# Inverse 16-point step of a spectral layer on 64x64 quarters of the array, two units at once, its outer level of signs moved to the finished rows

## The chip, the core and the metric

One core of a Trainium2 chip runs the whole program. The metric is the device time of one execution in microseconds, and smaller is better. Engines are named as the profile names them: PE (TensorE, matrix products), PEld (its weight loads), DVE (VectorE), ACT (ScalarE), POOL (GpSimd), SP (SyncE, which issues the transfers).

## The reference

The kernel adds a spectral layer and an MLP to its input. Sequence length S is 2048, width D is 512, hidden width F is 1792.

```python
xn = _layernorm(x, axis=-1)
# spectral part
X = jnp.fft.rfft2(xn, axes=(-2, -1)) * (w_r + 1j * w_i)
y = jnp.fft.irfft2(X, s=(S, D), axes=(-2, -1))
# MLP part
h = jnp.einsum("bsd,df->bsf", xn, w1) + b1
m = jnp.einsum("bsf,fd->bsd", h * jnp.tanh(softplus(h)), w2)
return x + y + m
```

## The kernel before

**Precision.** Every float32 operand is split into a float16 high and low half, and a product is three matmuls: high by high, high by low, low by high. The helper `mm3` (L61, L64, L65) issues them into one PSUM tile.

**The spectral part** does the Fourier transform along the sequence as 128 x 16 and goes through these steps: `s1_mm` (128-point transform for each of 16 residues s2), `p2_unit` (16-point step, PSUM tile psP2), `spectrum` (transform along the width into dre and dim, unpacking X, product with the weights w, result u), `dp_unit` (inverse along the width, psA, result `at`, moved into `ai` by four transfers), `ip_unit` (inverse 16-point step, psT, result `tt`, written to the DRAM array d_t by two transfers) and `s1_inverse` (inverse 128-point transform, psY, added into the output rows m or y). There are four chunks c of four units each, so 16 units of the 16-point steps, numbered 4c+g, and 16 calls of `s1_inverse`. `spectrum` runs twice for a chunk, for the even and the odd columns (par 0 and 1).

**An `ip_unit`** is three matmuls of 128 x 128 constants (`c_ip2`) against 512 columns of `ai`; the constants hold the whole 16-point transform. In its unit 0 one block of 128 columns has other constants, so that it has six matmuls. Its result leaves PSUM by an ACT operation (L626, high half) and a DVE operation (L627, low half).

**The MLP** runs as a row of half tiles. A half tile is `up(n)` (12 matmuls of 512 columns into ph, then the activation on ACT, hb and a, and the low half of a on DVE) or `down(n)` (12 matmuls of 512 columns into four tiles pa). There are 109 before the end, and the last four end the sum (pe). `mlp_end` adds pa into the rows m or y on DVE when a group of 512 rows is complete.

**The order** around the change is made by `stream_a` and a scheduler. `stream_a` is a generator that issues the spectral steps and yields their weights; after each yield the main loop issues as many MLP half tiles as keep the count of half tiles in step with the sum of the weights, so that `stream_a` ends at half tile B_END = 98. An `ip_unit` is issued when more than two units wait in the list `mid`. After it, `load_yi` issues 16 loads from d_t, one for each `s1_inverse`, and the calls of `s1_inverse` are spread over what is left of the half tiles, the first T_LAG = 5 of them behind. Engines take their instructions in program order. Tiles psP2, dre, dim, psA, psT and psY all use the PSUM pool ps_f, which has two buffers.

Of the kernel before, what the change touches and what calls it, by code (L numbers as in the profile page):

```python
# [19 lines left out]
P = 128  # L20
# [3 lines left out]
LAG = 2  # L24
N_UNITS = 101
LAST = 3
B_END = 98
T_LAG = 5
T_HOLD = 2


O_P2, O_IP2, O_D, O_I = 0, 512, 1024, 2048
N_CM = 3072


@with_exitstack
def spectral_mlp_kernel(ctx, tc, x, wt, w0, w1, b1, w2, cT, cIT, cM, out):
    nc = tc.nc
# [7 lines left out]
    tp = ctx.enter_context(tc.tile_pool(name="tp", bufs=1))  # L46
# [7 lines left out]
    outv = out.rearrange("(p s) d -> p s d", s=NS2)  # L54

    d_y1 = dp.tile([64, P, 256], F16, tag="d_y1", name="d_y1")
    d_t = dp.tile([P, 64, 256], F16, tag="d_t", name="d_t")

    def mm3(ps, stat, mov, start, stop, order=False):

        first = nc.tensor.matmul(ps, stat(0), mov(0), start=start, stop=False)  # L61
        if order:
            tc.keep_in_program_order(first)
        nc.tensor.matmul(ps, stat(0), mov(1), start=False, stop=False)  # L64
        nc.tensor.matmul(ps, stat(1), mov(0), start=False, stop=stop)  # L65
# [192 lines left out]
    sc = {}  # L258
# [180 lines left out]
    def load_yt(c, b, n=1):  # L439
        t = big.tile([P, 2, 4, 2, P], F16, tag="big", name=f"yt_{c}_{b}")  # L440
        w = 2048 // n
        for k in range(n):
            o = (2 * c + b) * 2048 + k * w
            tc.keep_in_program_order(
                nc.sync.dma_start(
                    t.rearrange("p g a h e -> p (g a h e)")[:, k * w : (k + 1) * w],
                    d_y1.rearrange("a (c f) e -> (a c) (f e)", c=2)[:, o : o + w],
                )
            )
        yts.setdefault(c, []).extend([t[:, 0], t[:, 1]])  # L450
# [161 lines left out]
                    at[:, k].rearrange("p h e -> p (h e)"),  # L612
                )

    def ip_unit(c, g):
        if True:
            fg = 4 * c + g
            ai = ait.pop(fg)
            ps = ps_f.tile([P, 4, P], F32, tag="f", name=f"psT_{fg}")
# [5 lines left out]
            tt = tp.tile([P, 4, 2, P], F16, tag="q2", name=f"tt_{fg}", bufs=3)  # L625
            nc.scalar.mul(tt[:, :, 0, :], ps, 2.0**-12)  # L626
            nc.vector.scalar_tensor_tensor(  # L627
                tt[:, :, 1, :], ps, 2.0**-12, tt[:, :, 0, :], op0=ALU.mult, op1=ALU.subtract
            )
            for c2 in range(2):  # L630
                f = 64 * c2 + 4 * fg
                nc.sync.dma_start(
                    d_t[f : f + 4].rearrange("f s e -> s f e"),
                    tt[64 * c2 : 64 * c2 + 64].rearrange("p l h e -> p l (h e)"),
                )


# [125 lines left out]
    def load_yi(todo):  # L763
        spots = []
        for tag in ("z", "u"):
            t = tp.tile([P, 4, 4, 2, P], F16, tag=tag, name=f"yi_{tag}")
            spots += [t[:, k] for k in range(4)]
        for k in range(4):
            t = tp.tile([P, 2, 4, 2, P], F16, tag=f"w{k}", name=f"yi_w{k}")
            spots += [t[:, 0], t[:, 1]]  # L770
        for (g, s), t in zip(todo, spots):
            nc.sync.dma_start(t.rearrange("p a h e -> p (a h e)"), d_t[:, 4 * (4 * g + s) : 4 * (4 * g + s) + 4].rearrange("p a e -> p (a e)"))
            yis.append(t)

    def s1_inverse(g, s):
        s2 = 4 * g + s
        yi = yis.pop(0)
        ps = ps_f.tile([P, 4, P], F32, tag="f", name=f"psY_{s2}")
        psr = ps.rearrange("p (b a) e -> p a b e", a=2)

        def slots(h, a):
            v = yi[:, :, h, :].rearrange("p (b a) e -> p a b e", a=2)[:, a]
            return v[:, :, ::-1] if a else v

        for a in range(2):
            mm3(psr[:, a], lambda h: sc["cIT"][:, s2, h, :], lambda h: slots(h, a), True, True, a == 0)
        psf = ps.rearrange("p a b -> p (a b)")
        if g in macc:
            m = macc[g][:, s, :]
            nc.vector.scalar_tensor_tensor(m, psf, sc["k"], m, op0=ALU.mult, op1=ALU.add)  # L790
            nc.sync.dma_start(outv[:, s2, :], m)
        else:
            if s % 2 == 0:
                sc["y"] = big.tile([P, 2, D], F32, tag="big", name=f"y_{s2}")
                nc.sync.dma_start(sc["y"], xv[:, s2 : s2 + 2, :])
            y = sc["y"][:, s % 2, :]
            nc.vector.scalar_tensor_tensor(y, psf, sc["k"], y, op0=ALU.mult, op1=ALU.add)
            yacc.setdefault(g, []).append(y)


# [7 lines left out]

    def stream_a():
        up_, mid = [], []  # L810
        load_yt(0, 0, 2)
        load_yt(0, 1, 2)
        for c in range(5):
            for g in range(4):
                if g in (1, 2) and c < 4:
                    load_wx(c, g - 1)
                if c < 4:
                    p2_unit(c, g)
                    yield 0.7
                if len(mid) > 2:  # L820
                    ip_unit(*mid.pop(0))
                    yield 0.7
            up_ += [(c - 1, g) for g in range(4)] if c else []
            if c == 1:
                load_it()
            if c < 4:
                for par in range(2):
                    if c < 3:
                        load_yt(c + 1, par)
                    for wgt in spectrum(c, par):  # L830
                        yield wgt
                        if up_:
                            u = up_.pop(0)
                            dp_unit(*u)
                            mid.append(u)
                            yield 0.7
                        elif len(mid) > 2:
                            ip_unit(*mid.pop(0))
                            yield 0.7
        while up_ or mid:  # L840
            if up_:
                u = up_.pop(0)
                dp_unit(*u)
                mid.append(u)
                yield 0.7
            if len(mid) > 2 or not up_:
                ip_unit(*mid.pop(0))
                yield 0.7

    ACT, DVE, POOL = nc.scalar, nc.vector, nc.gpsimd  # L850
# [409 lines left out]
def _dft_constants():  # L1260
# [11 lines left out]
    s = np.arange(16)  # L1272
# [109 lines left out]
```

## Time and profile before

| what | value |
|---|---|
| median of 3 runs | 370.63 us (370.26 to 370.74) |
| the profiled execution, its own time | 370.42 us |
| its span in the profile | 368.6 us |
| instructions | 5647 |
| PE, DVE, ACT, POOL busy | 362.0, 250.4, 171.6, 46.4 us |

The profile shows one execution. Its page gives busy times by engine, the span in 40 slices, the DMA queues, the chain of work that ended last, and the costliest groups of instructions; a row of a group reads line, engine, operation, output<-inputs, shapes and count, then busy time and the mean of one in ns, then the idle time of the engine just before and what ended it. A row of the timeline reads start, duration, engine, line, operation, tiles, shape and count; a wait stands in brackets with what ended it. A PE row's duration is longer than the distance to the next start, since matmuls are pipelined. Rows of SP (SPq) are issues of transfers. A row of the windows reads the stretch, its length, and for PE, PEld, DVE, ACT and POOL the busy time with the count, then the clock and the DMA share.

### The profile page before, as it was taken

To read this page: it belongs to the slowest core of one execution; us is meant where nothing else is said; L and a number is where in the kernel's file an instruction comes from. 1 tells how busy PE (TensorE), PEld (TensorE's weight loads), DVE (VectorE), ACT (ScalarE), POOL (GpSimd) and SP (SyncE) were. 2 spreads that over 40 slices of the span, in tenths; PEclk is the share of its full clock that TensorE was granted. 3 is DMA by queue.
4 is the path that set the end of the run, shared out by engine and by line. 5 is a ranking of instruction groups with operands and counts; after the bars stand their busy time and mean duration, and the time that the engine had idled before them with its cause. 6 is when DMAs were issued, how large, how long until landed. Compare 5 with 4: busy or idle time off the path is not lost.

```text
span 368.6 us, 5647 instructions
## 1 busy us (share of the span) xinstructions
PE 362.0 (98%) x2088; PEld 185.0 (50%) x2088; DVE 250.4 (68%) x474; ACT 171.6 (47%) x260; POOL 46.4 (13%) x49
## 2 busy tenths in 40 slices
PE   6999999999999999999999999999999999999996
PEld 2544445544544455444555454544545444445654
DVE  4898999643477654589887856877479944413454
ACT  5989968416335343342454354345435444422100
POOL 0020003202304200303030303030030300000000
PEclk9999999999999999999999999999999999999999
DMA  8935543896483488037202370106921234549554
GB/s 280 317 121 205 216 135 84 166 363 183 134 236 93 119 186 286 0 116 275 68 17 64 92 220 12 47 20 177 308 81 52 65 86 103 127 87 325 217 190 181
DMA packets 56011, 55.78 MB, mean 151 GB/s; under 512 B 16128, under 2 KB 44704, under 8 KB 55216
## 3 DMA queue, kind: packets, MB, share of 16 engines
q1 hardware_dynamic: 55984, 55.43, 49.7%
q8 instruction: 16, 0.26, 0.3%
q14 instruction: 11, 0.09, 0.1%
HBM read 35.46 MB, written 12.58 MB: 130 GB/s over the span
## 4 chain that ended last, share of the span: by engine, by line
PE 93%; DVE 2%; DMA 2%; SPq 1%; ACT 1%; issue 0%; ACTq 0%; DVEq 0%
PE ph L659 39%; PE pa L64 13%; PE pa L65 13%; PE pa L61 13%; PE psP L470 1%; PE psY L61 1%; DMA x<-in_x_dram 1%; PE psY L64 1%; PE psP L480 1%; PE psY L65 1%; PE psT L61 1%; DMA ai<-at 1%; PE psT L65 1%; PE psT L64 1%; PE psA L61 1%; PE psA L64 1%
## 5 line engine op out<-in xcount | busy, mean ns | idle before, releaser
L659 PE MATMUL ph<-xnT,w1t 128*128 128x512 f16 x672 | 153.7, 379 | 0.0
L659 PEld LDWEIGHTS <-w1t 128*128 128x128 f16 x672 | 65.0, 98 | 74.4 <-ACT w1t L304 0.3
L670 ACT ACTIVATE hb<-ph,b1t,fp_exp 128x512 f32<-128x512 f32 x56 | 43.2, 772 | 76.9 <-PE ph L659 76.9
L65 PE MATMUL pa<-w2t,a 128*128 128x512 f16 x181 | 68.6, 379 | 0.0
L61 PE MATMUL pa<-w2t,a 128*128 128x512 f16 x181 | 68.6, 379 | 0.0
L64 PE MATMUL pa<-w2t,a 128*128 128x512 f16 x181 | 68.6, 379 | 0.0
L682 DVE SCALAR_TENSOR_TENSOR a<-hb,ip_a,a 128x512 f16<-128x512 f32 x46 | 36.0, 783 | 35.9 <-ACT a L679 35.7
L679 ACT ACTIVATE a<-hb,ip_a 128x512 f16<-128x512 f32 x46 | 33.1, 719 | 2.2 <-DVE ip_a L243 1.2
L65 PEld LDWEIGHTS <-a 128*128 128x128 f16 x190 | 18.6, 98 | 21.1
L61 PEld LDWEIGHTS <-a 128*128 128x128 f16 x190 | 18.6, 98 | 19.3
L64 PEld LDWEIGHTS <-a 128*128 128x128 f16 x190 | 18.6, 98 | 19.0
L627 DVE SCALAR_TENSOR_TENSOR tt<-psT,tt 128x512 f16<-128x512 f32 x16 | 11.0, 687 | 17.7 <-ACT tt L626 17.7
L204 POOL TENSOR_TENSOR xh<-xs,xh 128x512 f16<-128x512 f32 x12 | 14.8, 1233 | 63.9 <-ACT xh L188 32.5
L485 DVE SCALAR_TENSOR_TENSOR z<-psP,z 128x512 f16<-128x512 f32 x16 | 10.9, 690 | 13.6 <-ACT z L484 13.6
L626 ACT ACTIVATE tt<-psT 128x512 f16<-128x512 f32 x16 | 9.5, 591 | 17.4 <-PE psT L65 13.9
L603 ACT ACTIVATE at<-psA 128x512 f16<-128x512 f32 x16 | 9.4, 589 | 17.0 <-PE psA L65 15.9
L379 ACT ACTIVATE u<-w,sc_u 128x512 f16<-128x512 f32 x16 | 10.8, 714 | 11.1 <-DVE w L579 7.0
L604 DVE SCALAR_TENSOR_TENSOR at<-psA,at 128x512 f16<-128x512 f32 x16 | 11.0, 687 | 7.2 <-ACT at L603 7.1
L188 ACT ACTIVATE xh<-x,nb,rs 128x512 f16<-128x512 f32 x12 | 9.7, 804 | 12.9 <-DVE nb L182 12.9
L484 ACT ACTIVATE z<-psP 128x512 f16<-128x512 f32 x16 | 9.5, 594 | 12.3 <-PE psP L480 12.3
L97 ACT ACTIVATE y<-psS 128x512 f16<-128x512 f32 x16 | 9.4, 588 | 11.3 <-PE psS L65 11.3
L98 DVE SCALAR_TENSOR_TENSOR y<-psS,y 128x512 f16<-128x512 f32 x16 | 11.0, 686 | 5.3 <-ACT y L97 5.3
(205 smaller groups left out, 569.7 us busy)
## 6 DMA issues: line engine op xcount, KB each, us to landing
wm<-in_wt_dram SPq DMA_DIRECT2D x8, 512.0 KB
ai<-at SPq DMA_DIRECT2D x64, 64.0 KB
d_t<-tt SPq DMA_DIRECT2D x32, 128.0 KB
w1s<-in_w_dram SPq DMA_DIRECT2D x7, 512.0 KB
w2s<-in_w_dram SPq DMA_DIRECT2D x7, 512.0 KB
d_y<-y SPq DMA_DIRECT2D x7, 512.0 KB
m<-in_x_dram SPq DMA_DIRECT2D x3, 1024.0 KB
yt<-d_y SPq DMA_DIRECT2D x6, 512.0 KB
```

Source lines behind the costliest of these rows:

```text
L61: first = nc.tensor.matmul(ps, stat(0), mov(0), start=start, stop=False)
L64: nc.tensor.matmul(ps, stat(0), mov(1), start=False, stop=False)
L65: nc.tensor.matmul(ps, stat(1), mov(0), start=False, stop=stop)
L98: nc.vector.scalar_tensor_tensor(y1v[:, :, 1, :], psv, 2.0**-17, y1v[:, :, 0, :], op0=ALU.mult, op1=ALU.subtract)
L204: engine.tensor_sub(self.xh[s][:, 1, :], self.xs[s], self.xh[s][:, 0, :])
L485: nc.vector.scalar_tensor_tensor(zl, psv, 2.0**-14, zh, op0=ALU.mult, op1=ALU.subtract)
L604: nc.vector.scalar_tensor_tensor(at[:, :, 1, :], ps, 2.0**-15, at[:, :, 0, :], op0=ALU.mult, op1=ALU.subtract)
L627: nc.vector.scalar_tensor_tensor(tt[:, :, 1, :], ps, 2.0**-12, tt[:, :, 0, :], op0=ALU.mult, op1=ALU.subtract)
L659: nc.tensor.matmul(ph[n + k], w1t[:, hw, dc, f * P : (f + 1) * P], xnT[g][:, hx, dc, :], start=(hw, hx, dc) == (0, 0, 0), stop=(hw, hx, dc ...
L670: nc.scalar.activation(hbt[n], ph.pop(n), AF.Mish, bias=b1t[:, f : f + 1], scale=s_exp[part_of(f)])
L679: nc.scalar.activation(act[n][:, 0, :], hbt[n], AF.Copy, scale=sc["a"])
L682: nc.vector.scalar_tensor_tensor(act[n][:, 1, :], hbt.pop(n), sc["a"], act[n][:, 0, :], op0=ALU.mult, op1=ALU.subtract)
```

## The change

The 16 calls of `ip_unit` become eight calls of `ip_pair`. The constants become two 64 x 64 blocks, one for each half r of the partitions of `ai`: each gives a part of the 16-point transform without its outermost sum and difference. A pair takes two units u. For each of the three products it issues four matmuls of 64 x 64 by 512 columns, one for each (u, r): the weights and `ai` from partition half r, the result into partition half u of the PSUM tile r. So a tile psT holds half r of both units and no longer one whole unit. Its two parts go to d_t[0] and d_t[1]. Unit 0's special block is six quarter matmuls of 128 columns more.

`load_yi` fetches the two parts for each `s1_inverse` with two transfers of 64 partitions where there was one of 128. `s1_inverse` has the same matmuls, and then adds the parts into the finished rows: the first part into both halves of 256 columns, the second with a plus into the lower and a minus into the upper half. That makes three DVE operations (512, 256 and 256 columns) where there was one (512). A scalar `nk` holds the negative factor.

The schedule changes too: `stream_a` ends at half tile 93, T_LAG is 4, a pair is issued behind the first `p2_unit` of a chunk or in `spectrum` where no `dp_unit` waits, and a yield of 0 ahead of each pair and behind it issues one half tile there.

```diff
-B_END = 98
-T_LAG = 5
+B_END = 93
+T_LAG = 4
...
+P2_AT, SP_AT = 0, 0
...
-    d_t = dp.tile([P, 64, 256], F16, tag="d_t", name="d_t")
+    d_t = dp.tile([2, 64, 64, 256], F16, tag="d_t", name="d_t")
...
-    c_ip2 = cMt[:, O_IP2 : O_IP2 + 512].rearrange("p (v h q) -> p v h q", v=2, h=2)
+    c_ip2 = cMt[:, O_IP2 : O_IP2 + 256].rearrange("p (v h q) -> p v h q", v=2, h=2)
...
+        sc["nk"] = scalars("nk", pW, -(2.0**-16))
...
-            if fg == 0:
-                mm3(ps[:, 0], lambda h: c_ip2[:, 1, h, :], lambda h: ai[:, 0, h, :], True, True, True)
-                mm3(ps[:, 1:4], lambda h: c_ip2[:, 0, h, :], lambda h: ai[:, 1:4, h, :], True, True)
-            else:
-                mm3(ps, lambda h: c_ip2[:, 0, h, :], lambda h: ai[:, :, h, :], True, True, True)
...
+    def ip_pair(c, g):
+
+        fgs = (4 * c + g, 4 * c + g + 1)
+        ai = [ait.pop(fg) for fg in fgs]
+        ps = [ps_f.tile([P, 4, P], F32, tag="f", name=f"psT_{fg}") for fg in fgs]
+        tiles = [(u, r) for u in (1, 0) for r in (1, 0)]
+        passes = ((0, 0), (0, 1), (1, 0))
+
+        def quarter(u, r, k, v, ls):
+            hc, hm = passes[k]
+            qs = slice(64 * r, 64 * r + 64)
+            return nc.tensor.matmul(
+                ps[r][64 * u : 64 * u + 64, ls],
+                c_ip2[qs, v, hc, :],
+                ai[u][qs, ls, hm, :],
+                start=k == 0,
+                stop=k == 2,
+            )
...
+        for k in range(3):
+            for t in tiles:
+                i = rest(k, *t)
...
+            for u in range(2):
+                f = 4 * fgs[u]
                 nc.sync.dma_start(
-                    d_t[f : f + 4].rearrange("f s e -> s f e"),
-                    tt[64 * c2 : 64 * c2 + 64].rearrange("p l h e -> p l (h e)"),
+                    d_t[r, f : f + 4].rearrange("f q e -> q f e"),
+                    tt[64 * u : 64 * u + 64].rearrange("p l h e -> p l (h e)"),
...
+            for c2 in range(2):
+                q = 32 * c2 + 2 * s2
+                nc.sync.dma_start(
+                    t[64 * c2 : 64 * c2 + 64].rearrange("p (r a) h e -> p r (a h e)", r=2),
+                    d_t[:, :, q : q + 2].rearrange("r f a e -> f r (a e)"),
+                )
...
+        def add_to(m):
+            mv = m.rearrange("p (b q) -> p b q", b=2)
+            nc.vector.scalar_tensor_tensor(
+                mv, psv[:, 0:1].to_broadcast((P, 2, 256)), sc["k"], mv, op0=ALU.mult, op1=ALU.add
+            )
+            for b, k in ((0, "k"), (1, "nk")):
+                nc.vector.scalar_tensor_tensor(mv[:, b], psv[:, 1], sc[k], mv[:, b], op0=ALU.mult, op1=ALU.add)
...
+        def pair():
+            yield 0
+            ip_pair(*mid.pop(0))
+            mid.pop(0)
+            yield 0
+            yield 1.4
...
+                if g == P2_AT and mid:
+                    yield from pair()
...
-                        elif len(mid) > 2:
-                            ip_unit(*mid.pop(0))
-                            yield 0.7
+                        elif n == SP_AT and len(mid) > 2:
+                            yield from pair()
...
+            if len(mid) > 3 or not up_:
+                yield from pair()
...
+        if not w:
+            half_tile()
+            continue
...
-        inv.append(np.einsum("dk,csaj->kajcsd", e, M).reshape(128, 128))
+        inv.append(
+            np.concatenate(
+                [np.einsum("dk,csaj->kajcsd", e[:2, 2 * r : 2 * r + 2], M).reshape(64, 64) for r in range(2)]
+            )
+        )
```

Before, PE did unit 8 like this, in the middle of the last chunk's work (psT is written from `ai` of the unit and the constants in cMt; w1t and xnT behind it belong to a half tile `up`):

```order
L61 LDWEIGHTS cMt_87
L61 MATMUL psT_8_3162<-ai_8_2897,cMt_87 128x512
L64 LDWEIGHTS cMt_87
L64 MATMUL psT_8_3162<-ai_8_2897,cMt_87 128x512
L65 LDWEIGHTS cMt_87
L65 MATMUL psT_8_3162<-ai_8_2897,cMt_87 128x512
L61 LDWEIGHTS a_3_2_2878
L61 MATMUL pa_3_0_3051<-w2t_90,a_3_2_2878 128x512
```

In the changed kernel units 8 and 9 stand together on PE, behind one half tile; the first pass and the first matmul of the second are shown:

```order
L628 LDWEIGHTS cMt_87
L628 MATMUL psT_9_3096<-ai_9_2944,cMt_87 64x512
L628 LDWEIGHTS cMt_87
L628 MATMUL psT_8_3095<-ai_9_2944,cMt_87 64x512
L628 LDWEIGHTS cMt_87
L628 MATMUL psT_9_3096<-ai_8_2896,cMt_87 64x512
L628 LDWEIGHTS cMt_87
L628 MATMUL psT_8_3095<-ai_8_2896,cMt_87 64x512
L628 LDWEIGHTS cMt_87
L628 MATMUL psT_9_3096<-ai_9_2944,cMt_87 64x512
```

Six rows for one unit, each matmul on 128 rows, have become 24 for two units, each on 64; the two tiles psT take turns, and both are written from both units.

DVE before, at the last `spectrum` (chunk 3, odd columns): X is unpacked from dre and es (a copy of dim), multiplied by the weights wO into w, summed, and written as u:

```order
L546 TENSOR_TENSOR X1_3_3077<-dre1_3_3067,es1_3_3075 128x256
L547 TENSOR_TENSOR X1_3_3077<-dre1_3_3067,es1_3_3075 128x256
L548 TENSOR_TENSOR X1_3_3077<-dre1_3_3067,es1_3_3075 128x256
L549 TENSOR_TENSOR X1_3_3077<-es1_3_3075,dre1_3_3067 128x256
L553 TENSOR_TENSOR w0_1_3_3109<-X1_3_3077,wO_3_2790 128x512
L627 SCALAR_TENSOR_TENSOR tt_6_3086<-psT_6_3082,tt_6_3086 128x4x128
L555 TENSOR_TENSOR w1_1_3_3110<-X1_3_3077,wO_3_2790 128x512
L559 TENSOR_TENSOR w2_1_3_3111<-w2_1_3_3111,w3_1_3_3112 128x512
L557 TENSOR_TENSOR w0_1_3_3109<-w0_1_3_3109,w1_1_3_3110 128x512
L682 SCALAR_TENSOR_TENSOR a_3_5_3106<-hb_3_5_3104,ip_a_379,a_3_5_3106 128x512
L567 TENSOR_TENSOR w1_1_3_3110<-w0_1_3_3109 128x4x64
```

DVE in the changed kernel at the same place; m_2 are the rows of group 2, to which `mlp_end` adds the four tiles pa:

```order
L548 TENSOR_TENSOR X1_3_3056<-dre1_3_3046,es1_3_3054 128x256
L549 TENSOR_TENSOR X1_3_3056<-dre1_3_3046,es1_3_3054 128x256
L550 TENSOR_TENSOR X1_3_3056<-dre1_3_3046,es1_3_3054 128x256
L551 TENSOR_TENSOR X1_3_3056<-es1_3_3054,dre1_3_3046 128x256
L732 SCALAR_TENSOR_TENSOR m_2_2718<-pa_2_1_2045,s_out_576,m_2_2718 128x512
L732 SCALAR_TENSOR_TENSOR m_2_2718<-pa_2_2_2046,s_out_576,m_2_2718 128x512
L732 SCALAR_TENSOR_TENSOR m_2_2718<-pa_2_3_2047,s_out_576,m_2_2718 128x512
L555 TENSOR_TENSOR w0_1_3_3137<-X1_3_3056,wO_3_2807 128x512
L557 TENSOR_TENSOR w1_1_3_3138<-X1_3_3056,wO_3_2807 128x512
L561 TENSOR_TENSOR w2_1_3_3139<-w2_1_3_3139,w3_1_3_3140 128x512
L706 SCALAR_TENSOR_TENSOR a_3_3_3092<-hb_3_3_3090,ip_a_379,a_3_3_3092 128x512
L651 SCALAR_TENSOR_TENSOR tt_8_3109<-psT_8_3095,tt_8_3109 128x4x128
```

The three rows m from pa_2_1 to pa_2_3 now stand between X and its products; before, `mlp_end` of that group stood ahead of X. The a and both tt of the pair now come between the products and their sum w0.

PE before, at the first unit that reads this u (psA of unit 12), with what stands ahead of it:

```order
L61 MATMUL psT_9_3205<-ai_9_2955,cMt_87 128x512
L64 LDWEIGHTS cMt_87
L64 MATMUL psT_9_3205<-ai_9_2955,cMt_87 128x512
L65 LDWEIGHTS cMt_87
L65 MATMUL psT_9_3205<-ai_9_2955,cMt_87 128x512
L61 LDWEIGHTS u_3_2834
L61 MATMUL psA_12_3214<-cMt_87,u_3_2834 128x128
L64 LDWEIGHTS u_3_2834
L64 MATMUL psA_12_3214<-cMt_87,u_3_2834 128x128
L65 LDWEIGHTS u_3_2834
```

PE in the changed kernel at the same unit, from its sixth matmul on:

```order
L66 MATMUL psA_12_3171<-cMt_87,u_3_2839 128x128
L62 LDWEIGHTS u_3_2839
L62 MATMUL psA_12_3171<-cMt_87,u_3_2839 128x128
L65 LDWEIGHTS u_3_2839
L65 MATMUL psA_12_3171<-cMt_87,u_3_2839 128x128
L683 LDWEIGHTS w1t_89
L683 MATMUL ph_3_5_3192<-xnT_3_1145,w1t_89 128x512
```

Before, unit 12 came whole behind a psT, with five half tiles between it and dim of the last `spectrum`; now the scheduler has put three matmuls of `up` into it, and it stands three half tiles, one pair and eight matmuls of a fourth behind dim.

More of the change, by code (lines that the diff above doesn't have):

```diff
@@ L613, in dp_unit, with rest @@
                 )
[L615 to L619, printed above, removed]
-            if fg == 0:
-                mm3(ps[:, 0], lambda h: c_ip2[:, 1, h, :], lambda h: ai[:, 0, h, :], True, True, True)
-                mm3(ps[:, 1:4], lambda h: c_ip2[:, 0, h, :], lambda h: ai[:, 1:4, h, :], True, True)
-            else:
-                mm3(ps, lambda h: c_ip2[:, 0, h, :], lambda h: ai[:, :, h, :], True, True, True)
-            tt = tp.tile([P, 4, 2, P], F16, tag="q2", name=f"tt_{fg}", bufs=3)
-            nc.scalar.mul(tt[:, :, 0, :], ps, 2.0**-12)
+    def ip_pair(c, g):
[14 more added lines that the diff above has]
+            )
+        def rest(k, u, r):
+            return quarter(u, r, k, 0, slice(1 if fgs[u] == 0 else 0, 4))
+        for k in range(3):
+            for t in tiles:
+                i = rest(k, *t)
+                if (k, t) == (0, tiles[0]):
+                    tc.keep_in_program_order(i)
+        if fgs[0] == 0:
+            for k in range(3):
+                for r in range(2):
+                    quarter(0, r, k, 1, slice(0, 1))
+        for r in range(2):
+            tt = tp.tile([P, 4, 2, P], F16, tag="q2", name=f"tt_{fgs[r]}", bufs=3)
+            nc.scalar.mul(tt[:, :, 0, :], ps[r], 2.0**-12)
@@ L771, in load_yi @@
         for (g, s), t in zip(todo, spots):
[L772 removed]
+            s2 = 4 * g + s
+            for c2 in range(2):
[4 more added lines that the diff above has]
+                )
             yis.append(t)
@@ L796, in s1_inverse @@
             y = sc["y"][:, s % 2, :]
-            nc.vector.scalar_tensor_tensor(y, psf, sc["k"], y, op0=ALU.mult, op1=ALU.add)
+            add_to(y)
             yacc.setdefault(g, []).append(y)
@@ L813, in stream_a @@
         for c in range(5):
-            for g in range(4):
-                if g in (1, 2) and c < 4:
+            for g in range(4 if c < 4 else 0):
+                if g in (1, 2):
                     load_wx(c, g - 1)
-                if c < 4:
-                    p2_unit(c, g)
-                    yield 0.7
-                if len(mid) > 2:
-                    ip_unit(*mid.pop(0))
-                    yield 0.7
+                p2_unit(c, g)
+                yield 0.7
+                if g == P2_AT and mid:
+                    yield from pair()
             up_ += [(c - 1, g) for g in range(4)] if c else []
@@ L829, in stream_a @@
                         load_yt(c + 1, par)
-                    for wgt in spectrum(c, par):
+                    for n, wgt in enumerate(spectrum(c, par)):
                         yield wgt
```

17 lines of the change are left out of this document (5 added, 12 removed).

## Prediction

> **What bounds the kernel now.** I read the page first: the busy shares, the granted clock and the shares of the chain that ended last.
>
> ```profile
> PE 362.0 (98%) x2088; PEld 185.0 (50%) x2088; DVE 250.4 (68%) x474; ACT 171.6 (47%) x260; POOL 46.4 (13%) x49
> ...
> PEclk9999999999999999999999999999999999999999
> ...
> PE 93%; DVE 2%; DMA 2%; SPq 1%; ACT 1%; issue 0%; ACTq 0%; DVEq 0%
> ```
>
> TensorE is the bound: it is busy for 98% of the span, at the full clock in every slice, and 93% of the chain is its own. A busy PE need not be at its peak, so the next view is the timeline around one inverse 16-point step (unit 15, PSUM tile psT; PEld is the weight load).
>
> ```profile
> 324.86 0.38 PE L61 MATMUL psT<-ai,cMt 128*128 128x512 f16 x1
> 324.87 0.10 PEld L64 LDWEIGHTS <-cMt 128*128 128x128 f16 x1
> 325.08 0.38 PE L64 MATMUL psT<-ai,cMt 128*128 128x512 f16 x1
> 325.08 0.10 PEld L65 LDWEIGHTS <-cMt 128*128 128x128 f16 x1
> 325.30 0.38 PE L65 MATMUL psT<-ai,cMt 128*128 128x512 f16 x1
> ...
> 325.51 0.38 PE L659 MATMUL ph<-xnT,w1t 128*128 128x512 f16 x1
> ```
>
> The reader should see three things. Starts are 0.216 us apart, so a unit holds PE for 3 x 0.216 = 0.65 us. A matmul's row lasts 0.38, so some 0.16 of each (its tail) lies under the next one. And a weight load starts with the matmul ahead of it and is over before that one ends: loads cost nothing here. Any PE time taken away shortens the kernel, unless PE then waits for something else.
>
> **What the change removes.** Sixteen units at 0.65 become eight pairs. A pair issues 12 matmuls on quarters of the array, three passes of four. If the four of a pass run side by side, a pass takes what one 512-column matmul takes, and a pair 3 x 0.216 = 0.65 where two units took 1.29. Eight times 0.65 is **5.2 us saved**. Unit 0 has a column block with other constants; here is what it costs now:
>
> ```profile
> 205.82 0.22 PE L61 MATMUL psT<-ai,cMt 128*128 128x128 f16 x1
> ...
> 205.99 0.33 PE L61 MATMUL psT<-ai,cMt 128*128 128x384 f16 x1
> ...
> 206.48 2.75 PE L659 MATMUL ph<-xnT,w1t 128*128 128x512 f16 x12
> ```
>
> Three 128-column matmuls take 0.17 and the unit 0.66 like any other. After the change its other columns run beside unit 1's full 512 and save nothing more, and six 128-column quarters, two at a time, add 0.17. The removal is worth **-5.0**.
>
> **Going into the quarters and out again.** The trace holds no matmul of 64 rows, so the price of a change of array shape, 16 in all, has to be bounded. Below: nothing, or a gain of nothing, since no work goes away with it. Above: the tail of the matmul ahead (0.16) and one weight load in the open (0.10), 0.26 each, 4.2 in all. Neither row is nearer than the other, so I take the middle, 0.13 each: **+2.1**, and a pair of 0.91.
>
> **A new wait, at the last spectrum.** The two order excerpts on DVE show it. The block that ends with u (the input of units 12 to 15) starts from the matmuls dim of PE, and these are its rows now in the timelines of PE, POOL, DVE and ACT:
>
> ```profile
> 287.32 0.38 PE L65 MATMUL dim<-z,cMt 128*128 128x512 f16 x1
> ...
> 289.24 1.27 POOL L554 TENSOR_TENSOR w<-X,wO 128x512 f32<-128x512 f32 x1 [16.10 <-issue]
> ...
> 289.35 0.41 DVE L549 TENSOR_TENSOR X<-es,dre 128x256 f32<-128x256 f32 x1
> 289.68 1.38 DVE L553 TENSOR_TENSOR w<-X,wO 128x512 f32<-128x512 f32 x1
> ...
> 290.46 1.72 POOL L556 TENSOR_TENSOR w<-X,wO 128x512 f32<-128x512 f32 x1
> ...
> 291.58 1.15 DVE L555 TENSOR_TENSOR w<-X,wO 128x512 f32<-128x512 f32 x1
> ...
> 293.26 0.68 DVE L557 TENSOR_TENSOR w<-w,w 128x512 f32<-128x512 f32 x1
> ...
> 295.19 0.41 DVE L569 TENSOR_TENSOR w<-w 128x256 f32<-128x256 f32 x1
> ...
> 295.70 1.34 ACT L379 ACTIVATE u<-w,sc_u 128x512 f16<-128x512 f32 x2 [0.89 <-DVE w L569]
> ...
> 279.59 2.07 DVE L708 SCALAR_TENSOR_TENSOR m<-pa,s_out,m 128x512 f32<-128x512 f32 x3
> ```
>
> Count from the start of the last dim. Now the upper halves of u are there at 295.70 + 1.34 - 287.32 = 9.7. After the change three rows m stand between X and w (last line: 2.07 for three). X ends at 2.4, m at 4.5. Both products then run mostly after POOL's two (1.9 to 4.9), so they cost 0.68 like the other wide ones and not 1.38 and 1.15: with some overlap left, 6.1. Then one wide sum (6.7), one a and two tt at 0.65 (8.7), the other sum (9.3), the quarter operations (third at 10.3) and ACT's two (11.65). PE, meanwhile, has 44 matmuls of 0.216, dim itself, the pair and six of 0.055 in front of the first matmul that reads this u: 9.5 + 0.2 + 0.91 + 0.33 = 10.95. It waits 0.7, and 0.2 more for a lower half, which DVE makes behind an a: **+0.9**. Bounds: 0, if DVE runs earlier than I add it up, and 2.5, if the products keep their old 1.38 and 1.15.
>
> **Other waits of PE.** Two go, both at psT in the stretch where SyncE issues the ai and d_t transfers back to back:
>
> ```profile
> 304.17 0.38 PE L65 MATMUL pa<-w2t,a 128*128 128x512 f16 x1
> 304.67 0.38 PE L61 MATMUL psT<-ai,cMt 128*128 128x512 f16 x1
> ...
> 311.89 0.38 PE L61 MATMUL pa<-w2t,a 128*128 128x512 f16 x1
> 312.54 0.38 PE L61 MATMUL psT<-ai,cMt 128*128 128x512 f16 x1 [0.27 <-DVE tt L627]
> ```
>
> The starts are 0.50 and 0.65 apart instead of 0.216: 0.28 + 0.43 = **-0.7**, since every pair now has a half tile (12 matmuls, 2.6) ahead of it and one behind. In exchange a pair takes both buffers of ps_f at once, and its transfers come in blocks (two groups of the page, a piece of the chain, a row of SyncE's timeline):
>
> ```profile
> L627 DVE SCALAR_TENSOR_TENSOR tt<-psT,tt 128x512 f16<-128x512 f32 x16 | 11.0, 687 | 17.7 <-ACT tt L626 17.7
> ...
> L626 ACT ACTIVATE tt<-psT 128x512 f16<-128x512 f32 x16 | 9.5, 591 | 17.4 <-PE psT L65 13.9
> ...
> 307.89 3.10 DMA ai<-at
> ...
> 314.73 2.51 SPq L610 DMA_DIRECT2D ai<-at  x4
> ```
>
> A buffer comes free behind an ACT and a DVE operation (0.6 and 0.7), the second one 0.6 later: 1.9 after the pair, which the half tile covers as long as neither engine has over half a microsecond queued. On SyncE the four stores of pair 10 and 11 (0.63 each) and the eight ai of units 14 and 15 stand in a row; counted from the end of that pair the stores end at 4.0, the first ai can start at 4.8 (behind psA of unit 14, ACT and DVE), and the last is issued at 9.8 and has landed by 12.9 at the 3.1 above, which is a landing in a crowd. The last pair starts at 3.9 + 3 x 2.6 + 0.9 = 12.6: covered but for 0.3. With psP2 and dim set at new places the cover will not hold everywhere; for some five places I take **+1.2**, between 0.3 (five at under 0.1) and 2.
>
> **The finished rows.** Every s1_inverse gets two more DVE operations of 256 columns, and the first keeps its 512.
>
> ```profile
> L790 DVE SCALAR_TENSOR_TENSOR m<-psY,sc_k,m 128x512 f32<-128x512 f32 x12 | 8.5, 743 | 4.6 <-PE psY L65 4.6
> L753 DVE SCALAR_TENSOR_TENSOR y<-pe,s_out,y 128x256 f32<-128x256 f32 x1 | 0.5, 483 | 0.2 <-PE pe L65 0.2
> ...
> 330.00:369.00 39.00, 35.25 (x228) 21.36 (x226) 17.34 (x26) 4.50 (x6) 0.00 (x0) 1.00 0.61 217
> ```
>
> 32 x 0.48 is at most 15.5 us of DVE, which in its last stage has 17.3 busy (the third sum of the last line) of 39, and the stage gets longer by five half tiles (13 us). PE hides it; without that cover a psY would wait about 1 us (two more operations) for its buffer. At the very end DVE has 2 us more to do while PE does its last 36 matmuls (nine of 512 columns, nine of 256, eighteen of 128: 1.9 + 1.0 + 1.0): **+0.2**, between 0 and 0.6. Loading the finished parts takes 32 transfers and not 16, on SyncE:
>
> ```profile
> 327.06 1.85 SPq L632 DMA_DIRECT2D d_t<-tt  x2
> 330.85 1.76 SPq L772 DMA_DIRECT2D yi_z<-d_t  x4
> ```
>
> At 0.44 an issue the extra sixteen cost SyncE 7 us, spread over the stage; the first unit needs one more issue and two more stores, some 2 us, and has five half tiles (13 us) before it, where it had three. Nothing, unless the loads are slow by several us.
>
> **Sum:** -5.0 + 2.1 + 0.9 - 0.7 + 1.2 + 0.2 = **-1.3**. The profiled execution took 370.42, which gives 369.1; the median of the runs is 370.63, 0.2 higher, so 369.1 to 369.3. About 0.2%, 0.74 us, is what a measurement can tell from no change.
>
> **Rivals.**
> *A, the quarters overlap but the array is emptied at each change and loads stand in the open.* Per pair the tail twice, and five loads (four for the quarters, one on the way out), of 0.05 to 0.10 since they have half the columns: 0.57 to 0.82, 4.6 to 6.5 in all. The wait at u shrinks to about 0.5. Sum +0.8 to +2.7: 371.2 to 373.1, slower. It decides from 0.21 per change on, where the sum is zero. For it: the loads' rows show them ahead of time only within one shape. Against it: the change between 128, 384 and 512 columns costs nothing above.
> The Trainium skill, page TensorEngine Tiling (Array Packing), Tiling Modes, Key Properties, says that changing the mode drains TensorE, and its Gotcha 2 that column tiling excludes the fast weight load; by that rule A holds. No row here shows it.
> *B, the waits eat the gain.* Half way to the upper bounds at u and at the other places (1.7 and 1.6) the sum is -0.1, 370.3, and at them (2.5 and 2) +1.1, 371.5: mostly no change. For it: DVE is the second busiest engine and gets 15 us more.
> *C, the change does not do what it says: quarters follow one another.* 96 x 0.216 = 20.7 instead of 10.4: +10.4 and more, some 382; if two of four overlap, nothing is saved and about 374. For it: no row shows two matmuls at once. Against it: the four read and write disjoint partitions and banks, so nothing in the program orders them.
> The Trainium skill, page TensorE: Matmul & The Clock Gate, Part 3, has packed matmuls of different tiles start about 4 ns apart; by it C falls and a pass is 0.23. No row here shows that either.
>
> **Chances.** Forecast (367.0 to 369.9) 0.57; A 0.20; B 0.15; C 0.08. The range reaches from 367.0 (no price for the change of shape, a wait at u of 1.1 since PE gets there sooner: -5.0 + 1.1 - 0.7 + 1.2 = -3.4) to 372.6; it leaves out C and the far end of A. Faster: the forecast, 0.57. Same: B and the near end of A, 0.15 + 0.02. Slower: 0.18 + 0.08 = 0.26.
>
> **What would show it.** The four quarter rows of a pass should start within 0.05 of one another and the next pass 0.22 later; from the first quarter to the next full matmul 0.65 to 1.2 (the row's start minus 0.216 of the one ahead gives the price in, the start of ph behind it the price out). The first psA of unit 12 that reads new u should start about 0.7 late. psT at 304 and 312 should start without a wait. DVE should be some 13 us busier after 325 with no psY late. Quarters 0.2 apart would be C; a pair over 1.3, A.

## The result, and the profile after

The changed kernel takes 368.24 us, the median of runs between 368.07 and 368.45; the kernel before takes 370.63 (370.26 to 370.74) beside it. The ratio is 0.9937, with an interval of 0.9920 to 0.9955. Run again beside the last experiments it took 368.78 (368.51 to 369.66), ratio 0.9954 (0.9940 to 0.9967). The forecast was 369.1, with a range of 367.0 to 372.6, and faster as the likeliest case. The result lies well inside that range, which was wide, near its fast end. The profiled execution took 368.08, its span 366.3; against 370.42 that is 2.34 less, where the sum said 1.3.

From the page of the changed kernel: the span, the busy shares, the granted clock, the chain that ended last by engine.

```profile
span 366.3 us, 5788 instructions
...
PE 360.1 (98%) x2139; PEld 182.3 (50%) x2139; DVE 259.7 (71%) x507; ACT 172.0 (47%) x260; POOL 45.8 (13%) x49
...
PEclk9999999999999999999999999999999999999999
...
PE 83%; DVE 11%; DMA 2%; ACT 2%; issue 1%; SPq 1%; ACTq 0%; DVEq 0%
```

PE is still the bound at the full clock. But the chain has 11% of DVE in it where it had 2%: part of the end time is now set by what PE waits for. The pair of units 10 and 11 in the timelines of PE and of the weight loads:

```profile
296.07 0.38 PE L66 MATMUL pa<-w2t,a 128*128 128x512 f16 x1
296.38 0.36 PEld L628 LDWEIGHTS <-cMt 64*64 64x64 f16 x12 [0.42 <-DMA ai<-at]
296.38 0.84 PE L628 MATMUL psT<-ai,cMt 64*64 64x512 f16 x12
...
297.15 2.12 PE L683 MATMUL ph<-xnT,w1t 128*128 128x512 f16 x9
```

And the same timeline of PE cut at 296.40, so that only what had started by then is in it:

```profile
296.38 0.41 PE L628 MATMUL psT<-ai,cMt 64*64 64x512 f16 x4
```

One quarter's row in a first pass is 0.40 long, and the row of the four together 0.41: they have started within 0.01 and run side by side. The first starts 0.31 behind the matmul ahead instead of 0.216, which is 0.09 on the way in. From it to the first full matmul behind the pair are 0.77, where three passes of 0.216 would be 0.65: 0.10 on the way out, and some 0.02 in the first pass. The pair costs 0.87 of PE, two units cost 1.29. The pair of units 0 and 1 has six more matmuls, those of 128 columns for unit 0's special block, and still lasts only 0.78, so they cost next to nothing:

```profile
203.98 0.85 PE L628 MATMUL psT<-ai,cMt 64*64 64x512 f16 x18
204.76 0.39 PE L62 MATMUL pa<-w2t,a 128*128 128x512 f16 x1
```

The last spectrum in the timelines of all engines; the last dim on PE starts the block:

```profile
278.39 0.38 PE L66 MATMUL dim<-z,cMt 128*128 128x512 f16 x1
...
280.81 0.41 DVE L551 TENSOR_TENSOR X<-es,dre 128x256 f32<-128x256 f32 x1
...
281.14 2.06 DVE L732 SCALAR_TENSOR_TENSOR m<-pa,s_out,m 128x512 f32<-128x512 f32 x3
...
283.12 0.68 DVE L555 TENSOR_TENSOR w<-X,wO 128x512 f32<-128x512 f32 x1
...
283.72 0.68 DVE L557 TENSOR_TENSOR w<-X,wO 128x512 f32<-128x512 f32 x1
...
288.57 1.33 ACT L380 ACTIVATE u<-w,sc_u 128x512 f16<-128x512 f32 x2 [0.44 <-DVE w L570]
...
289.95 0.23 PE L62 MATMUL psA<-cMt,u 128*128 128x128 f16 x1 [0.48 <-ACT u L380]
```

The three rows m stand where the order put them, both products take 0.68, and u's upper half is there 11.5 behind the last dim (288.57 + 1.33 - 278.39). PE stood ready at 289.31 (0.64 before 289.95) and waits; a lower half costs another 0.13 at 290.85.

The rest of PE's account, from the distances of its starts beyond what each matmul streams. In the order of time there are small waits at psP (0.15 at 146.6, 0.25 at 176.3, 0.15 at 218.9 and 259.7), at dim (0.35 at 199.6), and three of 0.06 at dre and dim: 1.23, where the kernel before had 0.35. One more wait lies inside the pair of units 12 and 13, which holds PE for 1.14 and not for 0.77, so 0.37 longer than the others:

```profile
303.78 1.22 PE L628 MATMUL psT<-ai,cMt 64*64 64x512 f16 x12
304.92 1.25 PE L683 MATMUL ph<-xnT,w1t 128*128 128x512 f16 x5
```

The two waits at psT (0.28 and 0.43), one of 0.14 at a psY and one of 0.06 at a psA are gone. Together: -5.2 for the quarters (8 x 0.65), +1.8 (8 x 0.22) for the changes of shape, +0.77 at u, +0.88 for the small waits, +0.37 in the pair, -0.91 for those that went: -2.3. PE's last matmul ends 2.13 earlier (363.12 against 365.25); the 0.2 that is left is spread over differences of single starts too small to pick out, about half of it before 50 us, where both kernels do the same work. The span behind the last matmul is 0.2 shorter.

### The profile page after: what moved, and what is told of

Its sections match the earlier page's. It is cut to its first block, busy times and chain, and to the rows that moved or that the text cites. A ratio compares the mean times of both kernels' runs of the same rounds, so it can differ in the third digit from the quotient of the medians.

```text
span 366.3 us, 5788 instructions
## 1 busy us (share of the span) xinstructions
PE 360.1 (98%) x2139; PEld 182.3 (50%) x2139; DVE 259.7 (71%) x507; ACT 172.0 (47%) x260; POOL 45.8 (13%) x49
## 4 chain that ended last, share of the span: by engine, by line
PE 83%; DVE 11%; DMA 2%; ACT 2%; issue 1%; SPq 1%; ACTq 0%; DVEq 0%
PE ph L683 34%; PE pa L66 12%; PE pa L65 12%; PE pa L62 12%; PE psT L628 2%; DMA ai<-at 1%; DVE m L732 1%; DMA x<-in_x_dram 1%; PE psP L472 1%; PE psY L65 1%; PE psY L66 1%; PE psY L62 1%; DVE a L706 1%; DVE at L606 1%; PE psP L482 1%
## 5 line engine op out<-in xcount | busy, mean ns | idle before, releaser
L706 DVE SCALAR_TENSOR_TENSOR a<-hb,ip_a,a 128x512 f16<-128x512 f32 x46 | 35.0, 761 | 40.4 <-ACT a L703 40.3
L556 POOL TENSOR_TENSOR w<-X,wE 128x512 f32<-128x512 f32 x4 | 5.1, 1270 | 68.6 <-DVE X L549 68.6
```

The source lines that it names most:

```text
L706: nc.vector.scalar_tensor_tensor(act[n][:, 1, :], hbt.pop(n), sc["a"], act[n][:, 0, :], op0=ALU.mult, op1=ALU.subtract)
```

## The experiments

Three questions: do the quarters make the gain, or the new order around them; what a change of shape costs; and what makes PE wait.

**1. The new order without the quarters.**

```diff
-        for k in range(3):
-            for t in tiles:
-                i = rest(k, *t)
...
+        for r in range(2):
+            mm3(ps[r], lambda h: c_p2[:, 0, h, :], lambda h: ai[r][:, :, h, :], True, True, True)
```

> The changed kernel's order, but each pair as six full-array matmuls, three a unit, with the forward step's constants (unit 0's own block left out, so the output is not the reference's). Theory (the quarters side by side make the gain, and waits of PE behind DVE take part of it): the matmuls of psT take 1.30 a pair instead of 0.87, 3.3 more in all with the price on the way in; PE comes later to the last u (waits 0.77 now), to dim at 199.6 (0.35) and to psP (0.25 and 0.15), and these waits shrink by 1.5 to 2 together: 369.5 (369.0 to 370.0). Rival (the new order makes the gain, the quarters none): 368.2 or less, with the waits as they are.

Measured 370.76 (370.68 to 370.96), ratio to before 1.0002 (0.9994 to 1.0011). Everything else of the change is in this kernel, the finished rows and their loads too, and without the quarters it is worth nothing: the gain needs them. The size was missed by 1.3, because of the waits. Those at psP and dim are as large as in the changed kernel (0.24 at 176.5, 0.34 at 199.7): they come with the order. Only the wait at u shrinks, from 0.77 to 0.31, and the 0.37 in the pair goes. PE's last matmul ends at 365.80, which is 2.68 behind the changed kernel.

**2. More changes of shape, with the same work.** Both kernels have three more full-array matmuls a pair; only their places differ.

```diff
+        def full(k):
+            return nc.tensor.matmul(ps[1], c_p2[:, 0, 0, :], ai[1][:, :, 0, :], start=True, stop=True)
+
         for k in range(3):
+            i = full(k)
...
             for t in tiles:
-                i = rest(k, *t)
+                rest(k, *t)
```

This is full_between. In full_ahead the three stand in a loop of their own ahead of the quarters.

> The changed kernel with three more full-array matmuls of 512 columns ahead of the twelve quarters of each pair, into the bank that the quarters then overwrite; every matmul starts and ends its own sum, so the output is not the reference's. Base for the next kernel. All theories: 0.65 more a pair, 5.2 in all, of which up to 2 is taken from waits: 371.7 (371.0 to 373.3), still two changes of shape a pair.

> The same matmuls as full_ahead, but one full-array matmul ahead of each pass of four quarters: six changes of shape a pair instead of two, 32 more in all; output as there. Theory (a change costs one weight load in the open, 0.09 to 0.10): 32 x 0.095 = 3.0 more than full_ahead (2.6 to 3.4). Rival A (the array is emptied at a change and the load stands open behind it, 0.26): 8.3 more. Rival D (the price belongs to the entry of a pair, its four loads or its wait for DMA, and not to a change): 0 to 0.8 more.

Measured 372.72 (372.63 to 373.03) and 376.36 (376.24 to 376.68): 3.64 for 32 changes, 0.11 each, where the theory had 2.6 to 3.4 in all. A pair of full_between in the timelines of PE and of the weight loads (L640 is the full matmul, L628 the quarters):

```profile
287.39 0.38 PE L640 MATMUL psT<-ai,cMt 128*128 128x512 f16 x1
287.70 0.41 PE L628 MATMUL psT<-ai,cMt 64*64 64x512 f16 x4
288.04 0.39 PE L640 MATMUL psT<-ai,cMt 128*128 128x512 f16 x1
288.36 0.41 PE L628 MATMUL psT<-ai,cMt 64*64 64x512 f16 x4
```

```profile
287.70 0.11 PEld L628 LDWEIGHTS <-cMt 64*64 64x64 f16 x4 [0.42 <-issue]
288.04 0.10 PEld L640 LDWEIGHTS <-cMt 128*128 128x128 f16 x1 [0.23 <-issue]
```

Full to quarters is 0.31 or 0.32 from start to start, quarters to full 0.34, against 0.216 within a shape. It is paid at every change, also where nothing is waited for, so it is no price of a pair's entry (rival D). Within one shape a load's row starts with the matmul ahead of it; across a change it starts with the first matmul of the new shape, and 0.09 to 0.10 is about the length of such a row (0.103 for a quarter, 0.096 for a full load). That the open load is the price, but for the 0.02 of a first pass, fits these numbers and was not tried by itself. At 0.26 a change (rival A) the difference would have been 8.3.

**3. The quarters in another order.**

```diff
-        for k in range(3):
-            for t in tiles:
+        for t in tiles:
+            for k in range(3):
```

> The changed kernel with the twelve matmuls of a pair in another order: all three of a quarter, then the next quarter (same sums). Theory (matmuls start in order, a quarter is held for 0.216, and two neighbours overlap only where they are on different quarters): nine steps of 0.216 instead of three, 1.30 more a pair, 10.4 in all less up to 2 of waits: 377 (375.5 to 378.8). Rival E (each quarter takes its matmuls by itself, so the order is free): 368.2. Rival F (quarters need all four loads of a pass together to overlap at all, else they follow one another): twelve steps, 15.5 more, 382 to 384.

Measured 368.62 (368.33 to 369.06): no slower than the changed kernel's 368.24 to 368.78. My theory was wrong by 8 us. The pair of units 8 and 9 in the timeline of PE:

```profile
282.94 0.86 PE L628 MATMUL psT<-ai,cMt 64*64 64x512 f16 x12
283.73 1.04 PE L683 MATMUL ph<-xnT,w1t 128*128 128x512 f16 x4
```

Twelve matmuls, three of one quarter after another in the program, and still 0.79 from the first to the full one behind them. The second matmul of a quarter does not hold up the first one of the next. The same timeline cut at 282.98 has four matmuls in it, started 0.01 apart, where those of the changed kernel are some 0.003 apart: the edit did change the order in which PE gets them, and all four quarters have begun before any has started its second matmul, 0.24 behind its first. So PE, which gets its instructions in program order, does not start them strictly in that order. It fits with this that unit 0's block costs next to nothing: a quarter of unit 0 has its 384 and 128 columns to do while one of unit 1 does 512.

**4. The wait at u.** Left out are the three rows m between X and the products.

```diff
         for s in range(4):
+            if g == 2 and s:
+                continue
```

> The changed kernel without three of the four DVE rows m<-pa of the third group of rows, those that stand between X and the products w of the last spectrum (their share of the sum is left out of the output). Theory (these rows make PE wait for u): DVE gets to the products 2.06 sooner, loses 1.2 of it since they then run beside POOL's two, and u is there 0.9 sooner; the waits of 0.64 and 0.13 at psA of unit 12 go, 367.5 (367.3 to 367.8). Rival (u is late for what stands on ACT and DVE behind the products, the rows of the pair and of a): waits as they are, 368.2.

Measured 368.12 (367.31 to 368.46). The wait at u falls from 0.77 to 0.38 and not to 0, and neither theory is right. The time hardly moves, since the pair of units 12 and 13 waited 0.96 here and 0.37 in the changed kernel. DVE in this kernel:

```profile
281.31 1.38 DVE L555 TENSOR_TENSOR w<-X,wO 128x512 f32<-128x512 f32 x1
282.61 1.75 DVE L557 TENSOR_TENSOR w<-X,wO 128x512 f32<-128x512 f32 x1
...
286.84 0.74 DVE L706 SCALAR_TENSOR_TENSOR a<-hb,ip_a,a 128x512 f16<-128x512 f32 x1
287.50 1.28 DVE L651 SCALAR_TENSOR_TENSOR tt<-psT,tt 128x512 f16<-128x512 f32 x2
288.70 1.40 DVE L381 SCALAR_TENSOR_TENSOR u<-w,sc_u,u 128x512 f16<-128x512 f32 x2
```

The products start 2.0 sooner, counted from the last dim (278.57 here), but now run beside POOL's two and take 1.38 and 1.75. They end 5.8 behind the last dim, where with the rows m they ended 6.0 behind it. So the rows m fill a time in which the products would have been slow. What makes u late beside them seems to be the a and the two tt of the pair: they stood between the wide sums, and now stand ahead of u's lower half, for which PE waits. The rows show this order; no run left those operations out.

**5. The finished rows.** Left out are the second and third operation on each; then the former two numbers of the table.

```diff
-            for b, k in ((0, "k"), (1, "nk")):
-                nc.vector.scalar_tensor_tensor(mv[:, b], psv[:, 1], sc[k], mv[:, b], op0=ALU.mult, op1=ALU.add)
```

> The changed kernel with only the first of the three DVE operations on each finished row; the odd half's part is left out of the output. DVE gets some 13 us less in the last stage. Theory (PE hides these operations, they count only behind the last matmul): 368.1 (367.7 to 368.4). Rival (DVE paces the last stage): 367.4 or less.

```diff
-B_END = 93
-T_LAG = 4
+B_END = 98
+T_LAG = 5
```

> The changed kernel with the former two numbers, B_END 98 and T_LAG 5: five more half tiles (13 us of PE) run before the finished rows and not beside them. Theory (the three operations on a finished row are free only while PE has a half tile or more between two psY): the last ones come late by 0.5 to 0.9 each, while the waits at u and dim go, 372 (370.5 to 373.5). Rival (the same matmuls, only in another order, DVE has room enough): 368.2 give or take 0.4.

Measured 368.71 (368.08 to 369.12) and 374.93 (374.80 to 375.12). The last stage of the changed kernel and then of the one with a single operation, in the table of busy times (PE, weight loads, DVE, ACT, POOL, clock, DMA share, GB/s):

```profile
325.00:340.00 15.00, 15.00 (x89) 8.55 (x88) 10.54 (x20) 3.67 (x5) 0.00 (x0) 1.00 0.69 202
340.00:369.00 29.00, 23.12 (x152) 13.96 (x150) 20.20 (x40) 1.50 (x2) 0.00 (x0) 0.99 0.41 151
```

```profile
325.00:340.00 15.00, 15.00 (x90) 8.59 (x88) 6.26 (x9) 4.02 (x6) 0.00 (x0) 1.00 0.70 200
340.00:369.00 29.00, 23.50 (x154) 14.12 (x152) 11.94 (x19) 1.50 (x2) 0.00 (x0) 0.99 0.44 158
```

DVE loses 12.5 us of work (10.54 + 20.20 to 6.26 + 11.94) and nothing is faster: PE hides it. The time is above the forecast of 367.7 to 368.4, in part since the wait in the pair of units 12 and 13, of which experiment 7 tells, was 0.64 in this kernel and 0.37 in the changed one; the rest is open. With the former numbers the half tiles that hide it are used up too early. PE and DVE near that kernel's end, in two timelines:

```profile
363.54 0.28 PE L62 MATMUL psY<-yi_w,cITt 128*128 128x256 f16 x1 [0.74 <-DVE m L825]
...
365.11 0.28 PE L62 MATMUL psY<-yi_w,cITt 128*128 128x256 f16 x1 [0.74 <-DVE m L825]
```

```profile
361.83 0.74 DVE L821 SCALAR_TENSOR_TENSOR m<-psY,sc_k,m 128x512 f32<-128x512 f32 x1
362.61 0.48 DVE L825 SCALAR_TENSOR_TENSOR m<-psY,sc_k,m 128x256 f32<-128x256 f32 x1
```

Here psY follows psY without a half tile between, each 1.57 behind the last, DVE's time for a finished row (about 0.78 and two of 0.40 from start to start). Six such waits, the last of them at pe, of 0.90 to 1.17 beyond PE's own pace are 5.8 us, and dre at 287.5 adds 1.17. So the two numbers belong to the change: they keep its second part, the level of signs on the finished rows, under cover.

**6. Another split of the half tiles.** B_END 96 and T_LAG 3; then T_HOLD 3 as well.

```diff
-B_END = 93
-T_LAG = 4
-T_HOLD = 2
+B_END = 96
+T_LAG = 3
+T_HOLD = 3
```

> The changed kernel with B_END 96 and T_LAG 3: three more half tiles before the finished rows. Theory (what is lost beside the price of the changes is waits of PE where a half tile too few stands ahead of DVE's work at dim and psP, and the three m rows at the last u): dim at 199.6 (0.35) and the wait at u (0.77) shrink, a wait for ai of some 0.2 comes at the pair of units 12 and 13, the end stays covered: 367.5 (366.8 to 368.3). Rival (the finished rows need the half tiles): 369 or more.

> table_96 with T_HOLD 3, so that the last finished rows come one half tile earlier. Theory (there PE ended 0.8 sooner than in the changed kernel, and DVE, with two finished rows back to back behind 354.8, gave 0.7 of it back at the end): last matmul at 362.3 as there, end 0.3 to 0.7 sooner: 367.7 (367.4 to 368.1). Rival (the end hangs on the stores that SyncE issues): 368.3 as before.

Measured 368.33 (367.82 to 368.54) and 367.75 (367.14 to 367.92). In both PE's last matmul ends 0.8 to 0.9 sooner than in the changed kernel (362.32 and 362.24): the wait at dim falls from 0.35 to 0.06, the one at u from 0.77 to 0.32, the 0.25 at psP goes, and a psY waits 0.2 at 328.3. But the spans are hardly shorter (366.2 and 366.1), and the first kernel's 368.33 lies just above its forecast. In the second kernel DVE's last row ends at 362.63, before the changed kernel's at 363.51, and SyncE's last stores are issued earlier by 0.8:

```profile
361.28 1.95 SPq L778 DMA_DIRECT2D out_dram<-y  x4
```

In the changed kernel:

```profile
362.24 1.82 SPq L778 DMA_DIRECT2D out_dram<-y  x4
```

From the end of the last issue to the end of the span it is 2.8 in the second kernel and 2.2 in the changed one; why, no run shows. The table with T_HOLD 3 is the fastest of these kernels, ratio 0.9918 (0.9904 to 0.9931), below the changed kernel's beside it (0.9954, 0.9940 to 0.9967). Against its first measurement (0.9920 to 0.9955) the intervals overlap.

**7. The wait inside the pair of units 12 and 13.** The quarters of a pass would start together, so all that the pair lasts beyond 0.77 is lost: 0.37 in the first profile of the changed kernel, 0.64 in one_add, 0.96 in no_m2, and 1.03 when the changed kernel was run again. The expectations count only the distance between the first two starts beyond some 0.23, and so have 0.14, 0.40, 0.73 and 0.79 for the same waits.

> The changed kernel as it is, beside the next two on the same chip: 368.2 (367.9 to 368.6); its wait inside the pair of units 12 and 13, 0.14 to 0.40 in the runs so far, shows how far the landing of ai varies.

Measured 368.78 (368.51 to 369.66), a little above what was expected.

In no_m2 the four ai transfers of unit 13 were then given to ACT's queue, to see whether they come too late:

```diff
-                nc.sync.dma_start(
+                (nc.scalar if fg == 13 else nc.sync).dma_start(
                     ai[32 * k : 32 * k + 32].rearrange("q l h e -> q l (h e)"),
```

> no_m2 with the four ai transfers of unit 13 issued by ACT and not by SyncE. Theory (with the wait at u gone, PE waits for ai of unit 13 since SyncE needs 8.0 for the eight issues of units 12 and 13): the wait of 0.73 inside the pair of units 12 and 13 falls to 0.2 or less, 367.5 (367.2 to 367.8). Rival (the transfers themselves are late, or ACT, held by its issues, makes psT or psA late): 368.1 with another wait of 0.4 or more.

Measured 369.38 (369.17 to 369.50), slower by over 1 us. The four issues hold ACT for 3.25, tt of the pair comes 2.3 later, the next psA waits 1.09 for its bank, and the pair still waits 0.63. This theory fell. The rows of the changed kernel, run again, show what it is:

```profile
300.03 2.60 SPq L656 DMA_DIRECT2D d_t<-tt  x4
...
303.33 0.60 ACT L605 ACTIVATE at<-psA 128x512 f16<-128x512 f32 x1 [1.10 <-DMA d_t<-tt]
...
303.96 0.69 DVE L606 SCALAR_TENSOR_TENSOR at<-psA,at 128x512 f16<-128x512 f32 x1 [1.01 <-ACT at L605]
...
304.70 0.84 PE L628 MATMUL psT<-ai,cMt 64*64 64x512 f16 x11 [0.63 <-DVE at L606]
```

One quarter has started at 303.67; the next waits until DVE has finished at of unit 15 (303.96 + 0.69 = 304.65), which frees the second PSUM bank. That at is late since ACT waits for one of the three buffers that at and tt share, which a store of tt empties; and those stores stand on SyncE behind eight ai issues. So at was given other buffers:

```diff
-            at = tp.tile([P, 4, 2, P], F16, tag="q2", name=f"at_{fg}", bufs=3)
+            tag, bufs = ("X", 2) if fg > 13 else ("q2", 3)
+            at = tp.tile([P, 4, 2, P], F16, tag=tag, name=f"at_{fg}", bufs=bufs)
```

> The changed kernel, but with at of units 14 and 15 in the two buffers of X, which is done with by then, instead of the three that at and tt share; every engine has the same instructions in the same order. Theory (inside the pair of units 12 and 13 PE waits not for ai but for the PSUM bank that at of unit 15 frees, and ACT writes that at only when a d_t store has emptied its buffer): ACT's second at follows the first within 0.8, the wait of 0.14 to 0.79 falls below 0.1, and the time no longer scatters with it: 367.9 (367.6 to 368.2). Rival (ai of unit 13 lands late): the wait stays, 368.2 to 368.8.

Measured 367.96 (367.83 to 368.35), ratio 0.9928 (0.9913 to 0.9943). From this kernel's timelines of ACT and of PE:

```profile
301.54 1.07 ACT L606 ACTIVATE at<-psA 128x512 f16<-128x512 f32 x2
```

```profile
303.93 0.84 PE L629 MATMUL psT<-ai,cMt 64*64 64x512 f16 x12
```

Both at follow one another, the twelve quarters are one row of 0.84, and the wait is gone. SyncE issues the ai of units 12 and 13 until 299.9, as when the changed kernel was run again, so a late ai was not the cause. The time is 0.3 below the changed kernel's first measurement and 0.8 below its second, where the profiles had 0.37 and 1.03 of this wait; the intervals of the ratios overlap, with the second (0.9940 to 0.9967) only just, so the profile shows the wait gone better than the times show what it is worth.

## Why the prediction held, point by point

- **Quarters side by side (-5.0): right, and 0.2 too little.** The first pass starts within 0.01 and a pair streams for 0.65, which is -5.2. The step added 0.17 for unit 0's six small matmuls, as if they had to follow the others two at a time; their pair lasted 0.78, like the rest. The Trainium skill, page TensorE: Matmul & The Clock Gate, Part 3 (packed matmuls start about 4 ns apart), agrees: rows of 0.40 make one of 0.41 for four, some 3 ns apart. Rival C falls.
- **Sixteen changes of shape (+2.1): right in kind, a little too high.** 0.11 each, 1.8 in all, and 0.11 again over 32 added changes. The middle of the bounds was taken for want of a nearer row, so that it came this close is in part luck; the upper bound had added the tail to a load in the open, and only about the load's length shows. Rival A, which decided from 0.21, falls. The Trainium skill, page TensorEngine Tiling (Array Packing), Tiling Modes, Key Properties, says that a change of mode drains TensorE. The trace agrees in that every change costs time, but the new shape's first row starts at 296.38 while the row ahead, modelled, lasts until 296.45.
- **The wait at u (+0.9): right, 0.77.** The count of DVE's rows came out within 0.2 us (u at 11.5, forecast 11.65; PE ready at 10.9, forecast 10.95). But the rows m are not the whole cause, as the step put it: without them half of the wait stays.
- **Two waits at psT gone (-0.7): both went, and 0.2 at a psY and a psA with them, but it is not the whole story.** The step covered ai of units 14 and 15 and each bank by one ACT and one DVE operation. It did not see that at and tt share three buffers, so that a store stuck on SyncE holds up a PSUM bank. That brought back 0.37 to 1.03 at the pair of units 12 and 13.
- **Other waits (+1.2): 0.9**, at psP and dim, from the order and not from the quarters (the first experiment).
- **The finished rows (+0.2): -0.2**, the difference of what lies behind the last matmul (3.4 before, 3.2 after); DVE is 12.0 busier after 325 (18.78 to 30.74, forecast 13), and the cover was real. Without it a psY waits 0.9 to 1.17, where "about 1" was said.
- **Rival B** (waits eat the gain) was a matter of size. All waits that came, less those that went, are 1.1 in the profile on record (0.77 + 0.88 + 0.37 - 0.91), where the forecast had 1.4.

The forecast was 1.0 too slow: 0.2 from unit 0's block, 0.3 from the price of the changes, 0.1 at u, 0.3 at the other waits, 0.4 at the end and 0.2 from the waits that went beside those at psT. Against that stand the 0.37 in the pair, which no term had, and the 0.2 of small differences. Of 5.2 us freed on PE, 1.8 go to the changes of shape and 1.1 to waits.

## What to carry to other kernels

Packing small matmuls pays only in blocks: count the changes of shape (0.11 each here), and keep the packed ones together. Work taken from an engine that is 98% busy comes back only in part, because the engines that it outran set new waits; count those rows one by one, as for u here, and look at which tiles share buffers with a queued store, not only at the tile that is waited for. Work moved to another engine was free here only while the table left cover beside it: with the former numbers the kernel took 6 to 7 us more.

## What was not expected of the hardware

- The quarters take their matmuls each by itself: three in a row for one quarter, then the next, cost the same as one for each in turn (0.79 against 0.77 a pair).
- A quarter's weight load of 64 x 64 lasts 0.106 at the median, no less than a full one of 128 x 128 (0.098).
- A DMA issue on ACT's queue held ACT for as long as it would SyncE's: 3.25 for the four ai of unit 13, 3.20 on SyncE in the changed kernel, and ACT had work waiting behind them.
- Leaving out 2.06 us of DVE rows just ahead of two products brought the end of these 0.2 nearer to the last dim, as they ran beside POOL's and took 1.38 and 1.75 and not 0.68.
